# Transposes of the attention outputs: from TensorE through PSUM to DMA on 16-bit planes

## The chip, the cores and the metric

The kernel runs on one core of a Trainium2 chip as one launch. The metric is the device time of an execution in microseconds (us); lower is better. The kernel before takes 1124.64 us, the median of three runs (1124.45 to 1126.33).

## The reference

Attention with pooled queries feeds a channel-mixing MLP; all arrays are float32.

```python
# q, k, v: (8 batches, 8 heads, 1152, 64); x below: (8, 576, 512)
q_pool = q.reshape(B, H, S // 2, 2, D).mean(axis=3)          # 576 rows a head
scores = np.matmul(q_pool, k.transpose(0, 1, 3, 2)) / np.sqrt(D)
attn = softmax(scores)                                       # max subtracted, sum + 1e-9
x = np.matmul(attn, v).transpose(0, 2, 1, 3).reshape(B, 576, H * D)
x_prev = x shifted by one row (zeros ahead)
xk, xr = mu_k * x + (1 - mu_k) * x_prev, mu_r * x + (1 - mu_r) * x_prev
k = np.maximum(xk @ w_k, 0.0)                                # w_k 512 x 1024
out = sigmoid(xr @ w_r) * (k * k @ w_v)                      # w_v 1024 x 512, w_r 512 x 512
```

## The kernel before, in words

Every product is computed from fp16 pairs (a high part and a remainder), which is why each matrix product appears as several matmuls.

*Attention.* A head `n` (0 to 63) has six blocks of 96 pooled queries, 384 blocks in all. In `block`, TensorE (PE) writes the scores of a block into one of three PSUM tiles `s` (line 586), VectorE (DVE) takes the row maximum over keys into `mx` (593), PE transposes `mx` (596), DVE reduces again into `mb` (598), PE spreads it (625), ScalarE (ACT) writes it as an extra row of `qT` (628), PE adds the low score products (602), ACT takes the exponential into `pf` (635), and GpSimd (POOL) makes the low part `pl` from it (643). `window` multiplies 128 rows of weights with `v` (693, 695, 700) into the one PSUM bank `a`; `halves` (664) does the half window that two heads of a pair share.

*The pair's end.* Two heads form a pair; a batch has four pairs, the program 32. After the last window of a head, DVE (716, 718) takes the reciprocal of the sums and line 725 (721 on ACT in the first heads) normalises bank `a` into the SBUF tile `xb`, ten units of 64 columns. After the second head, `turns` runs: POOL copies one unit (734), PE transposes five 128x128 float32 pieces of `xb` into bank `a` (741), three, then two, and each group is copied from the bank into `xt` (750): a 64x64 and a 128x256 piece by ACT and a 64x64 piece by DVE from the first, a 128x256 piece by ACT from the second. The bank is taken until those copies are done. `xt` holds a batch transposed, channels on partitions, and has three buffers.

*MLP.* `ff` mixes tiles of 256 rows of `xt` (`mix`: 933, 936, 941, 944) and multiplies them with the weights (all at line 965), with `r`, `g` and `gl` between (992, 994, POOL 996). The weights are decoded in the first part of the program (836 to 854).

*The order.* Nothing is issued where it is written. Every operation is recorded with its engine, an estimated duration and its buffers (`op`), a planner (`Issue.run`) lays them out, a table of random moves (`MOVES`, with `SEED`) nudges the layout, and then each engine gets its instructions in that order. All engines work strictly through their own list. All loads, stores and DMA transposes are issued by SyncE (SP): loads (469, 515), transposes of keys and queries (535, 491), the copy `ks2` of the transposed keys (538) that the low score products read, stores (1032).

`SPREAD_MAX` is 0 and `NARROW` 32 in the kernel before, so the branches that they choose (`weigh`, `spread`) issue no instruction.

Of the kernel before, what the change touches and what calls it, by code (L numbers as in the profile page):

```python
# [11 lines left out]
F32 = mybir.dt.float32  # L12
F16 = mybir.dt.float16
# [8 lines left out]
P = 128  # L22
# [16 lines left out]
ROW = "Prelu"  # L39

# [12 lines left out]
KN_POOL, VT_POOL, XL_POOL = 0, 0, 0  # L53
# [7 lines left out]
SPREAD_MAX = 0  # L61
# [11 lines left out]
FIX_ACT = 1  # L73
FIX = 0.07
# [3 lines left out]
NARROW = 32  # L78
# [11 lines left out]
SEED, SPREAD = 2, 1.0  # L90
# [227 lines left out]
def kernel(  # L318
# [73 lines left out]
    vb = bufs("vb", NV, [P, NC, D + 8], F16)  # L392
# [3 lines left out]
    den, xb = bufs("den", 2, [P, NW], F32), bufs("xb", 1, [P, 2 * NW + 4, D], F32)  # L396
    xl_b = bufs("xlb", 1, [P, 3, D], F32)
# [29 lines left out]
    for t_ in qn:  # L427
        nc.gpsimd.memset(t_[:, 1, :, D:P] if SPREAD_MAX else t_[:, 1, :, 0:D], 0.0)
# [19 lines left out]
    def queries(n, key):  # L448
# [3 lines left out]
        l0 = 0 if n < SPREAD_MAX else D  # L452
# [57 lines left out]
    def prep(n, key):  # L510
# [26 lines left out]
        if n >= SPREAD_MAX:  # L537
            op("DMA", 0.54, lambda: nc.sync.dma_start(ks2[i][D:P], ks1[i][0:D]),
               r=[("ks1", i), ("ks1", i, 5)], w=[("ks2", i)], key=key + 1, load=0.65, more=0.15)
# [25 lines left out]
    def block(n, j, i, t):  # L565
# [10 lines left out]
        mxz, mbz = mx[z], mb[z]  # L576
# [12 lines left out]
        for c0, c1 in BK:  # L589
# [15 lines left out]
        if n < SPREAD_MAX:
            for c0, c1 in BK:
                op("PE", (c1 - c0) * 0.0430, lambda c0=c0, c1=c1: scores2(c0, c1),
                   r=[("ks1", hp), ("ks1", hp, 5)] + kl, w=[("s", z)], key=t + O_MAX)
            if FIX_ACT:
                op("ACT", 0.07, lambda: nc.scalar.activation(mbz, mbz, getattr(AF, ROW), scale=1.0 + EPS,  # L610
                                                             alpha=(1.0 - EPS) / (1.0 + EPS)),
                   r=[("mb", z)], w=[("mb", z)], key=t + O_MAX)
            else:
                op("DVE", FIX, lambda: nc.vector.scalar_tensor_tensor(
                    mbz, mbz, (1.0 + EPS) / (1.0 - EPS), mbz, op0=ALU.mult, op1=ALU.max),
                   r=[("mb", z)], w=[("mb", z)], key=t + O_MAX)

            def spread():
                for c0, c1 in BK:
                    nc.tensor.matmul(cols(c0, c1), mbz.broadcast_to([P, P]), negd[:, 0:c1 - c0].rearrange("p c q -> p (c q)"),  # L620
                                     start=False, stop=True, skip_group_check=True)

            op("PE", NC * QN / 2400 + 0.012, spread, r=[("mb", z)], w=[("s", z)], key=t + O_EXP)
        else:
            op("PE", 0.047, lambda: nc.tensor.matmul(s[:, 0:QN], mbz.broadcast_to([P, P]), negi[:, P - QN:P],  # L625
                                                     start=False, stop=False, skip_group_check=True),
               r=[("mb", z)], w=[("s", z)], key=t + O_MAX)
            op("ACT", 0.153, lambda: nc.scalar.activation(qlo[0:1], s[0:1, 0:QN], getattr(AF, ROW),  # L628
                                                          scale=1.0 - EPS, alpha=(1.0 + EPS) / (1.0 - EPS)),
               r=[("s", z)] + kl, w=qm, key=t + O_MAX)  # L630

            for c0, c1 in BK:
                op("PE", (c1 - c0) * 0.0430, lambda c0=c0, c1=c1: scores2(c0, c1),
                   r=[("ks2", hp)] + kl + qm, w=[("s", z)], key=t + O_EXP)
# [24 lines left out]
    def halves(n, t):  # L659
# [15 lines left out]
        x_ = xl_b[0][:, 0]  # L675
# [4 lines left out]
    def window(n, w, t):  # L680
# [72 lines left out]

    VW, MID = 2 * D + 1, NW - 1
    ROUND = [(0, 1, 2), (MID + 1, MID - 1, MID), (MID + 2, MID + 3, MID + 4)]
    UNIT = {MID: 2 * NW + 3, **{x: 2 * x + 2 for x in range(MID)}, **{MID + 1 + x: 2 * x + 3 for x in range(MID)}}

    def weigh(g, m, t):


        if m == MID:
            ps = [(2 * g, 0, HW, TQ), (2 * g + 1, HW, P, 0)]
        else:
            ps = [(2 * g + int(m > MID), 0, P, HW + (m if m < MID else m - MID - 1) * P)]
        us = [x for _, x0, x1, p0 in ps for x in range(p0 // U, (p0 + x1 - x0) // U)]
        pfk, plk = [("pf", x) for x in us], [("pl", x) for x in us]
        r_, y = [(r_, o.index(m)) for r_, o in enumerate(ROUND) if m in o][0]
        a0 = y * VW
        order = sorted(ROUND[r_])
        vk = [(x, n % NV, c0) for n, *_ in ps for x in ("vt", "vtl") for c0 in (0, *V_CUT)]  # L770
        k = range(NC)

        def mms(src, vs, c0, c1, v0):
            for c in range(c0, c1):
                for n, x0, x1, p0 in ps:
                    nc.tensor.matmul(a_b[x0:x1, a0 + v0:a0 + VW], src[:, c, p0:p0 + x1 - x0],
                                     vs[n % NV][:, c, 0:VW - v0],
                                     start=(m == order[0] and c == 0 and v0 == 0), stop=(v0 > 0 and c == NC - 1),
                                     skip_group_check=True)

        first = m == order[0]
        steps = [(0, 3), (3, 6), (6, NC)] if len(ps) == 1 else [(0, NC)]
        for c0, c1 in steps:
            op("PE", HALF * 0.65 if len(ps) > 1 else 3 * 0.0582, lambda c0=c0, c1=c1: mms(half(pf, F16, 1), vt, c0, c1, 0),
               r=vk + pfk + ([] if first and c0 == 0 else [ka]), w=[ka], key=t)
        for c0, c1 in [(0, 5), (5, NC)] if len(ps) == 1 else [(0, NC)]:
            op("PE", HALF * 0.35 if len(ps) > 1 else (c1 - c0) * 0.0306, lambda c0=c0, c1=c1: mms(pl, vb, c0, c1, D),
               r=[("vb", n % NV) for n, *_ in ps] + plk + [ka], w=[ka], key=t)
        if m < order[-1]:
            return  # L790

        b, h = divmod(2 * g, H)
        u = a_b[:, 0:3 * VW].rearrange("p (k x) -> p k x", x=VW)
        dz, x_ = den[r_ % 2][:, 0:3], xl_b[0]
        us = [UNIT[x] for x in ROUND[r_]]
        step = us[1] - us[0]
        op("DVE", 0.075, lambda: nc.vector.tensor_scalar(dz, u[:, :, 2 * D], GUARD, None, op0=ALU.add),
           r=[ka], w=[("den", r_ % 2)], key=t + O_EVAC)
        op("DVE", 0.08, lambda: nc.vector.reciprocal(dz, dz), r=[("den", r_ % 2)], w=[("den", r_ % 2)], key=t + O_EVAC)
        op("ACT", 0.051 + 3 * D / 1200, lambda: nc.scalar.copy(x_, u[:, :, 0:D]), r=[ka], w=[("xlb",)], key=t + O_EVAC)  # L800
        op("DVE", 0.07 + 3 * D / 960, lambda: nc.vector.tensor_tensor(
            u[:, :, D:2 * D], u[:, :, D:2 * D], x_, op=ALU.add), r=[ka, ("xlb",)], w=[ka], key=t + O_EVAC)
        op("DVE", 0.07 + 3 * D / 960, lambda: nc.vector.tensor_tensor(
            xb[0][:, us[0]:us[2] + 1:step], u[:, :, D:2 * D], dz.unsqueeze(2).broadcast_to([P, 3, D]), op=ALU.mult),
           r=[("den", r_ % 2), ka], w=[("xb", x) for x in us], key=t + O_EVAC)
        if r_ < 2:
            return
        turns(b, h // 2, 2 * NW + 2, t)
# [312 lines left out]
```

## Time and profile before

| what | value |
|---|---|
| median of three runs | 1124.64 us |
| span of the profiled execution | 1123.9 us |
| PE busy | 1086.5 us (97%) |
| DVE, ACT, POOL busy | 898.8, 841.5, 538.8 us |
| TensorE's granted clock, mean | 0.999 |

The span runs from the first to the last instruction; the execution that was profiled has no device time of its own in the results, so its span is set beside the median of the runs, which is 0.74 us longer. Busy is the union of the engine's instruction records. PE is the matmul itself, PEld the load of its stationary operand, which runs beside it. Matmuls overlap, so a record is longer than the distance from one matmul to the next.

### The profile page before, as it was taken

How to read it: one execution, taken by the hardware profiler on the slowest of the kernel's cores; microseconds unless marked ns; L12 is line 12 of the kernel's file. 1: busy time of each engine (PE TensorE's matmuls, PEld its weight loads, DVE VectorE, ACT ScalarE, POOL GpSimd, SP SyncE). 2: the span in 40 equal slices, each digit the busy share in tenths (PEclk: the TensorE clock that was granted, in tenths of full speed). 3: DMA queues.
4: the chain of work that ended last, by engine and by line, in shares of the span. 5: the costliest groups of instructions: out<-in, count | busy, mean ns of one | idle time of the engine just before them, and what ended most of it. 6: DMA issues, size and time to landing. Idle time of an engine off the chain costs nothing.

```text
span 1123.9 us, 44399 instructions
## 1 busy us (share of the span) xinstructions
PE 1086.5 (97%) x18956; PEld 891.4 (79%) x18956; DVE 898.8 (80%) x1660; ACT 841.5 (75%) x1794; POOL 538.8 (48%) x579
## 2 busy tenths in 40 slices
PE   6888899999999999999999999999999999999998
PEld 5777778888797878888697888888797978787565
DVE  7999979998987998789878788888878787874530
ACT  7999987778777687777867677778777776765743
POOL 4566665544364444555454544545453544542111
PEclk9999999999999999999999999999999999999999
DMA  8999756674455635553465454455564423410000
GB/s 207 260 208 210 170 102 145 160 149 101 105 119 127 128 69 119 101 132 100 87 146 107 103 118 102 104 128 98 120 123 102 89 76 76 75 28 11 20 20 29
DMA packets 218742, 125.69 MB, mean 112 GB/s; under 512 B 154032, under 2 KB 190896, under 8 KB 218544
## 3 DMA queue, kind: packets, MB, share of 16 engines
q1 hardware_dynamic: 218544, 122.86, 49.6%
q8 instruction: 148, 2.42, 0.9%
q14 instruction: 50, 0.41, 0.1%
HBM read 67.11 MB, written 9.44 MB: 68 GB/s over the span
## 4 chain that ended last, share of the span: by engine, by line
PE 53%; DVE 1%; issue 0%; ACT 0%; ACTq 0%; DVEq 0%
PE f L965 21%; PE s L602 6%; PE s L586 6%; PE s L965 4%; PE a L695 3%; PE a L700 3%; PE a L693 3%; PE a L965 2%; PE a L664 1%; PE s L596 1%; PE s L625 1%; PE a L741 1%; DVE mx L593 0%; DVE xlr L944 0%; DVE qn L480 0%
## 5 line engine op out<-in xcount | busy, mean ns | idle before, releaser
L643 POOL TENSOR_SCALAR pl<-pf 128x864 f16<-128x864 uint16 x384 | 382.1, 995 | 422.0 <-ACT pf L635 380.0
L593 DVE TENSOR_REDUCE mx<-s 128x96 f16<-128x864 f32 x384 | 400.8, 1053 | 78.9 <-PE s L586 49.0
L635 ACT ACTIVATE pf<-s 128x864 int32<-128x864 f32 x384 | 335.8, 883 | 84.7 <-PE s L602 60.3
L586 PE MATMUL s<-qT,ks 128*128 128x96 f16 x3456 | 224.0, 206 | 12.5 <-ACT pf L635 8.9
L602 PE MATMUL s<-qT,ks 128*128 128x96 f16 x3456 | 216.2, 206 | 2.9 <-ACT qT L628 2.7
L586 PEld LDWEIGHTS <-ks 128*128 128x128 f16 x3456 | 184.1, 98 | 40.4 <-issue 13.6
L602 PEld LDWEIGHTS <-ks 128*128 128x128 f16 x3456 | 179.2, 98 | 21.9 <-issue 4.0
L695 PE MATMUL a<-vt,pf 128*128 128x64 f16 x2304 | 192.3, 194 | 0.3 <-issue 0.3
L693 PE MATMUL a<-vt,pf 128*128 128x65 f16 x2304 | 191.8, 193 | 0.1
L693 PEld LDWEIGHTS <-pf 128*128 128x128 f16 x2304 | 161.2, 99 | 4.0 <-issue 0.4
L695 PEld LDWEIGHTS <-pf 128*128 128x128 f16 x2304 | 155.0, 97 | 4.7 <-issue 0.2
L628 ACT ACTIVATE qT<-s 1x96 f16<-1x96 f32 x384 | 87.2, 230 | 82.5 <-PE s L625 79.4
L598 DVE TENSOR_REDUCE mb<-s 128x1 f16<-128x128 f32 x384 | 109.1, 286 | 36.8 <-PE s L596 29.6
L965 PE MATMUL f<-xhk,wk_hi 128*128 128x256 f16 x496 | 135.2, 273 | 0.1
L965 PE MATMUL f<-xhk,wk_lo 128*128 128x256 f16 x496 | 135.2, 273 | 0.0
L965 PE MATMUL f<-xlk,wk_hi 128*128 128x256 f16 x496 | 135.2, 272 | 0.0
L700 PE MATMUL a<-vb,pl 128*128 128x65 f16 x2304 | 123.2, 193 | 0.8 <-issue 0.5
L996 POOL TENSOR_TENSOR gl<-g 128x512 f16<-128x512 f32 x72 | 76.1, 1057 | 88.3 <-ACT g L994 85.5
L965 PEld LDWEIGHTS <-wk_hi 128*128 128x128 f16 x1152 | 106.0, 98 | 10.2 <-issue 0.2
L700 PEld LDWEIGHTS <-pl 128*128 128x128 f16 x2304 | 97.6, 98 | 6.4 <-issue 0.6
L965 PE MATMUL f<-wv_hi,gl 128*128 128x512 f16 x240 | 91.0, 379 | 0.0
L965 PE MATMUL f<-wv_lo,g 128*128 128x512 f16 x240 | 90.9, 379 | 0.0
(117 smaller groups left out, 1988.4 us busy)
## 6 DMA issues: line engine op xcount, KB each, us to landing
kr<-in_k_dram SPq DMA_DIRECT2D x64, 288.0 KB
vr<-in_v_dram SPq DMA_DIRECT2D x64, 288.0 KB
qr<-in_q_dram SPq DMA_DIRECT2D x63, 256.0 KB
ks<-ks SPq DMA_DIRECT2D x64, 144.0 KB
out_dram<-em SPq DMA_DIRECT2D x36, 256.0 KB
xt<-in_moe_w_k_dram SPq DMA_DIRECT2D x8, 512.0 KB
xt<-in_moe_w_v_dram SPq DMA_DIRECT2D x8, 512.0 KB
qr<-in_q_dram SPq DMA_DIRECT2D x32, 64.0 KB
```

The costliest lines, as they stand in the source:

```text
L586: nc.tensor.matmul(cols(c, c + 1), ks1[hp][:, c, :], qhi, start=(c == c0), stop=False, skip_group_check=True)
L593: op("DVE", 0.975, lambda: nc.vector.tensor_reduce(mxz[:, P - QN:P], grid(0, NC).rearrange("p c q -> p q c"), axis=AX.X, op=ALU.max), r=[( ...
L598: op("DVE", 0.199, lambda: nc.vector.tensor_reduce(mbz, s[:, 0:P], axis=AX.X, op=ALU.max), r=[("s", z)], w=[("mb", z)], key=t + O_MAX)
L602: nc.tensor.matmul(cols(c, c + 1), (ks1 if n < SPREAD_MAX else ks2)[hp][:, c, :], qlo, start=False, stop=True, skip_group_check=True)
L628: op("ACT", 0.153, lambda: nc.scalar.activation(qlo[0:1], s[0:1, 0:QN], getattr(AF, ROW), scale=1.0 - EPS, alpha=(1.0 + EPS) / (1.0 - EPS) ...
L635: op("ACT", NC * QN / 1200 + 0.06, lambda: nc.scalar.activation(pf[:, :, rows], grid(0, NC), AF.Exp, bias=SHIFT, scale=0.125 / (2.0 * SQ)) ...
L643: op(pe, d, lambda: en.tensor_scalar(pl[:, :, rows], half(pf, U16, 0)[:, :, rows], LO, 1.0, op0=ALU.mult, op1=ALU.mult), r=[("pf", x) for ...
L693: nc.tensor.matmul(bank[:, a0:a0 + VN], half(pf, F16, 1)[:, c, rows], vt[jv][:, c, D:D + VN], start=(w == 1 and c == 0 and hh == 0), stop= ...
L695: nc.tensor.matmul(bank[:, a0:a0 + D], half(pf, F16, 1)[:, c, rows], vt[jv][:, c, 0:D], start=False, stop=False, skip_group_check=True)
L700: nc.tensor.matmul(bank[:, a0:a0 + VN], pl[:, c, rows], vb[jv][:, c, 0:VN], start=False, stop=(c == NC - 1), skip_group_check=True)
L965: nc.tensor.matmul(ps, terms[i][0], terms[i][1], start=(first and i == 0), stop=(i == last), skip_group_check=True)
L996: op("POOL", 2 * n * 0.00203 + 0.08, lambda f2=f2: nc.gpsimd.tensor_tensor(gl[:, f2, 0:n], g32[:, f2, 0:n], gh[:, f2, 0:n], op=ALU.subtrac ...
```

## The change

For pairs 5 to 31 (`CROSS = range(4, 31)`, counted from 0) `turns` hands over to `crossed`. POOL copies `xb`, seen as 16-bit words, into two planes `xp` (low halves and high halves), in two instructions. One DMA transpose on SP turns all ten 128x128 pieces of the two planes into `xd`. Three copies join the planes in `xt`: two of 64 partitions by ACT, one of 128 partitions by POOL. PE and bank `a` have no part in it. Pairs 1 to 4 and 32 keep the old way.

Beside that: `mx` has two buffers in place of three; the constant `negd` (one POOL instruction at the start), the unused branches and some spare columns are dropped; and the planner's table of moves is another one with another seed, so that every engine's list is laid out anew.

```diff
+CROSS = range(4, 31)
+SPLIT_ENG = "POOL"
+JOIN_ENG = "POOL"
+HALF_ENG = 'ACT'
+CROSS_LOAD, CROSS_MORE = 2.1, 0.5
...
-    44, 69, 70, 101, 134, 152, 174, 178, 265, 338, 388, 440, 473, 536, 539, 701, 728, 899, 906, 1027, 1054,
...
+    19, 49, 186, 236, 290, 409, 442, 580, 720, 1033, 1106, 1276, 1618, 2283, 5078, 5201, 6339, 9039, 9106,
...
-SEED, SPREAD = 2, 1.0
+SEED, SPREAD = 37, 1.0
...
-    mx, mb = bufs("mx", 3, [P, P], F16), bufs("mb", 3, [P, 1], F16)
+    mx, mb = bufs("mx", 2, [P, P], F16), bufs("mb", 3, [P, 1], F16)
+    xp, xd = bufs("xp", 1, [P, 2, 2 * NW, D], U16)[0], bufs("xd", 1, [P, 2, NW, P], U16)[0]
...
+    def crossed(b, g, t):
+        xu = xb[0].bitcast(U16).rearrange("p u (d t) -> p t u d", t=2)
+        yu = xt[b % 3][:, g].bitcast(U16).rearrange("p (q t) -> p t q", t=2)
+        for u1, u0, n_ in ((1, 1, 2 * NW - 1), (0, 1, 1)):
+            d, f = copier(SPLIT_ENG, 2 * D * n_)
+            op(SPLIT_ENG, d, lambda f=f, u0=u0, u1=u1, n_=n_: f(xp[:, :, u1:u1 + n_], xu[:, :, u0:u0 + n_]),
+               r=[("xb", x) for x in range(u0, u0 + n_)], w=[("xp", u1)], key=t + O_TURN)
+        op("DMA", 0.5, lambda: nc.sync.dma_start_transpose(
+            xd.rearrange("p t k x -> p (t k) x"), xp.rearrange("p t u d -> p (t u d)")),
+           r=[("xp", 0), ("xp", 1)], w=[("xd",)], key=t + O_TURN, load=CROSS_LOAD, more=CROSS_MORE)
+        free = [("xtf",)] if b % 3 == 2 else []
+        for y, ps, k0, k1, x0, x1, e in ((0, slice(0, HW), 0, 1, 0, HW, HALF_ENG), (1, slice(HW, P), 0, 1, HW, P, HALF_ENG),
+                                         (2, slice(0, P), 1, NW, 0, P, JOIN_ENG)):
+            n_ = (k1 - k0) * (x1 - x0)
+            d, f = copier(e, 2 * n_)
+            q0 = SPAN[y][0]
+            op(e, d, lambda f=f, ps=ps, k0=k0, k1=k1, x0=x0, x1=x1, n_=n_, q0=q0: f(
+                yu[ps, :, 1 + q0:1 + q0 + n_].rearrange("p t (k x) -> p t k x", k=k1 - k0), xd[ps, :, k0:k1, x0:x1]),
+               r=[("xd",)] + free, w=[("xt", b % 3, g, y)] + [("xt", b % 3, g, 3)] * (y == 2), key=t + O_TURN)
...
+        if b * NG + g in CROSS:
+            return crossed(b, g, t)
```

The order at the end of pair 13 shows the moved work on three engines. Line numbers differ between the two programs; the names of tiles carry buffer numbers.

PE before, at the first of the two groups of transposes: the pair's last score matmul, the transposes of `xb` into bank `a`, the transpose of `mx` of a later block, and MLP matmuls.

```order
L586 MATMUL s_133<-qT_88,ks_1_84 128x96
L741 MATMUL a<-ident,xb_105 128x128 x3
L596 LDWEIGHTS mx_99
L596 MATMUL s_135<-identb,mx_99 128x128
L965 LDWEIGHTS g_0_117
L965 MATMUL f<-wv_hi,g_0_117 128x512
```

PE of the change, between the last window of pair 13 and the first of pair 14 (593 is the transpose of `mx`, 913 the MLP, 583 the scores).

```order
L913 MATMUL f<-xhk_114,wk_hi 128x256
L593 LDWEIGHTS mx_96
L593 MATMUL s_132<-identb,mx_96 128x128
L913 LDWEIGHTS wk_hi
L913 MATMUL f<-xlk_112,wk_hi 128x256
L913 LDWEIGHTS wk_lo
L913 MATMUL f<-xhk_114,wk_lo 128x256
```

No transpose of `xb` stands there; MLP and score matmuls follow one another up to the next pair's window.

POOL before, at the same pair's end: 643 makes `pl`, 558 a part of `v`, 734 copies one unit of `xb`.

```order
L643 TENSOR_SCALAR pl<-pf 128x9x96
L734 COPY xb_105<-xb_105 128x64
L643 TENSOR_SCALAR pl<-pf 128x9x96 x7
L558 TENSOR_SCALAR vb_94<-vr_75 128x9x64
```

POOL of the change there: 719 are the two split copies, 730 the join, 619 makes `pl`, 944 makes `gl`.

```order
L719 COPY xp_104<-xb_102 128x2x576
L619 TENSOR_SCALAR pl<-pf 128x9x96 x2
L719 COPY xp_104<-xb_102 128x2x64
L944 TENSOR_TENSOR gl_117<-g_0_116 128x512
L619 TENSOR_SCALAR pl<-pf 128x9x96
L944 TENSOR_TENSOR gl_117<-g_0_116 128x512
L730 COPY xt_106<-xd_105 128x2x512
L619 TENSOR_SCALAR pl<-pf 128x9x96 x2
```

Three copies stand where one stood, with `pl` and `gl` queued between and behind them.

SP before, near the same pair: the transpose of keys (535), their copy `ks2` (538), loads and a store.

```order
L515 DMA vr_74<-in_v_dram 128x576
L535 DMA_TRANSPOSE ks_0_83<-kn_79 128x9x128
L538 DMA ks_0_85<-ks_0_83 64x1152
L515 DMA kr_73<-in_k_dram 128x576
```

SP of the change: 533 is the transpose of keys, 721 that of the planes, 535 the copy of the keys.

```order
L533 DMA_TRANSPOSE ks_0_81<-kn_77 128x9x128
L721 DMA_TRANSPOSE xd_105<-xp_104 128x10x128
L535 DMA ks_0_83<-ks_0_81 64x1152
L513 DMA vr_73<-in_v_dram 128x576
```

The new transpose stands between the keys' transpose and their copy, and what follows it on SP waits for it to be issued.

## Rows read from the trace of the kernel before

**Rows 1.** The page: span, and busy time of each engine.

```profile
span 1123.9 us, 44399 instructions
PE 1086.5 (97%) x18956; PEld 891.4 (79%) x18956; DVE 898.8 (80%) x1660; ACT 841.5 (75%) x1794; POOL 538.8 (48%) x579
```

**Rows 2.** Stretches: length, busy us of PE, PEld, DVE, ACT, POOL; clock, DMA.

```profile
0.00:150.00 150.00, 121.93 (x2536) 107.21 (x2537) 132.22 (x243) 138.50 (x305) 93.64 (x101) 1.00 0.92 209
150.00:1036.00 886.00, 880.43 (x15898) 732.90 (x15897) 737.73 (x1360) 658.03 (x1395) 432.73 (x466) 1.00 0.48 104
1036.00:1124.00 88.00, 84.16 (x526) 51.25 (x524) 28.86 (x58) 45.01 (x96) 12.47 (x12) 0.99 0.07 25
```

**Rows 3.** Line 741, the transposes: duration ns min/median/max.

```profile
L741 PE MATMUL a<-ident,xb x160: 272/273/329, 44.3 to 1036.2; 128*128 128x128 f32 x160
```

**Rows 4.** Timeline around the two groups of pair 31: start us, length us.

```profile
1007.68 0.51 PE L741 MATMUL a<-ident,xb 128*128 128x128 f32 x3
...
1008.03 0.55 PE L586 MATMUL s<-qT,ks 128*128 128x96 f16 x9
...
1010.22 0.38 PE L741 MATMUL a<-ident,xb 128*128 128x128 f32 x2
...
1010.43 0.21 PE L625 MATMUL s<-negi,mb 128*128 128x96 f16 x1
```

**Rows 5.** Waits of PE and PEld, 150 to 1036 us: total, times, longest.

```profile
PE s L625 <- DVE mb L598: 2.9, 5, 1.0
...
PE a L741 <- DVE xt L750: 0.5, 1, 0.5
...
PEld L625 <- DVE mb L598: 5.9, 11, 1.2
...
PEld a L741 <- DVE xt L750: 1.4, 4, 1.0
```

**Rows 6.** Groups by form: busy us, mean ns, idle before. Copies out of bank a.

```profile
L750 ACT COPY xt<-a 128x256 f32<-128x256 f32 x64 | 23.3, 365 | 3.1 <-PE a L741 1.3 <-PE s L625 1.1 <-DVE em L1029 0.4
...
L750 DVE COPY xt<-a 64x64 f32<-64x64 f32 x32 | 7.3, 228 | 4.3 <-ACT xt L750 3.4
```

**Rows 7.** Three POOL lines: duration ns min/median/max.

```profile
L643 POOL TENSOR_SCALAR pl<-pf x384: 910/911/1893, 15.8 to 1026.9; 128x864 f16<-128x864 uint16 x192
...
L558 POOL TENSOR_SCALAR vb<-vr x56: 670/670/1056, 93.2 to 989.8; 128x576 f16<-128x576 f32 x56
...
L996 POOL TENSOR_TENSOR gl<-g x72: 1038/1040/1510, 141.7 to 1106.0; 128x512 f16<-128x512 f32 x72
```

**Rows 8.** Groups of `pl` on POOL and of its reader on PE, as above.

```profile
L643 POOL TENSOR_SCALAR pl<-pf 128x864 f16<-128x864 uint16 x384 | 382.1, 995 | 422.0 <-ACT pf L635 380.0 <-PE s L602 11.4 <-PE a L700 6.3
...
L700 PE MATMUL a<-vb,pl 128*128 128x65 f16 x2304 | 123.2, 193 | 0.8 <-issue 0.5 <-POOL pl L643 0.3
```

**Rows 9.** Two DVE lines, two SBUF inputs: groups (mean ns), then min/median/max.

```profile
L547 DVE SCALAR_TENSOR_TENSOR vt<-vr,vt 128x576 f16<-128x576 f32 x64 | 59.0, 922 | 1.3 <-ACT vt L543 1.3
...
L944 DVE TENSOR_TENSOR xlr<-xm,xhr 128x256 f16<-128x256 f32 x72 | 39.6, 558 | 4.2 <-ACT xhr L941 3.9
...
L547 DVE SCALAR_TENSOR_TENSOR vt<-vr,vt x64: 718/752/1596, 15.1 to 992.2; 128x576 f16<-128x576 f32 x64
...
L944 DVE TENSOR_TENSOR xlr<-xm,xhr x72: 390/418/1204, 121.5 to 1092.0; 128x256 f16<-128x256 f32 x72
```

**Rows 10.** Timeline of SP: the keys' transpose, the copy behind it.

```profile
323.50 1.29 SPq L535 DMA_TRANSPOSE ks<-kn  x1
...
327.75 0.47 SPq L538 DMA_DIRECT2D ks<-ks  x1
```

**Rows 11.** Timeline near 512 us: start, length, idle before, releaser.

```profile
511.90 2.29 POOL L643 TENSOR_SCALAR pl<-pf 128x864 f16<-128x864 uint16 x2 [1.25 <-ACT pf L635]
...
511.93 1.48 DVE L480 SCALAR_TENSOR_TENSOR qn<-qs,qn 128x576 f16<-128x576 f32 x1
...
513.80 0.22 PE L625 MATMUL s<-negi,mb 128*128 128x96 f16 x1 [0.98 <-DVE mb L598]
```

More of the change, by code (lines that the diff above doesn't have):

```diff
@@ L52 @@
 LATE, SLACK = 0.04, 0.05
-KN_POOL, VT_POOL, XL_POOL = 0, 0, 0
+KN_POOL = 0
+XL_POOL = 0
 DEC_K, DEC_RV = "V", "V"
@@ L427 @@
     for t_ in qn:
-        nc.gpsimd.memset(t_[:, 1, :, D:P] if SPREAD_MAX else t_[:, 1, :, 0:D], 0.0)
+        nc.gpsimd.memset(t_[:, 1, :, 0:D], 0.0)
     for t_ in mx:
@@ L451, in queries @@
         i, u = n // 2 % 2, n // 2 % N_QN
-        l0 = 0 if n < SPREAD_MAX else D
+        l0 = D
         qv = q[b, h:h + 2].rearrange("h (t f) d -> h t (f d)", f=2)
@@ L536, in prep @@
                r=[(x, m, c) for x in ("kn", "knl") for c, _ in KC], w=[("ks1", i), ("ks1", i, 5)], key=key + 1, load=1.9, more=T_MORE)
-        if n >= SPREAD_MAX:
-            op("DMA", 0.54, lambda: nc.sync.dma_start(ks2[i][D:P], ks1[i][0:D]),
-               r=[("ks1", i), ("ks1", i, 5)], w=[("ks2", i)], key=key + 1, load=0.65, more=0.15)
+        op("DMA", 0.54, lambda: nc.sync.dma_start(ks2[i][D:P], ks1[i][0:D]),
+           r=[("ks1", i), ("ks1", i, 5)], w=[("ks2", i)], key=key + 1, load=0.65, more=0.15)
         for c0, c1 in zip((0, *V_CUT), (*V_CUT, NC)):
@@ L575, in block @@
         rows, us = slice(p0, p0 + QN), range(p0 // U, (p0 + QN) // U)
-        mxz, mbz = mx[z], mb[z]
+        mxz, mbz, y = mx[i % 2], mb[z], i % 2
         def cols(c0, c1):
@@ L601, in scores2 @@
             for c in range(c0, c1):
-                nc.tensor.matmul(cols(c, c + 1), (ks1 if n < SPREAD_MAX else ks2)[hp][:, c, :], qlo,
+                nc.tensor.matmul(cols(c, c + 1), ks2[hp][:, c, :], qlo,
                                  start=False, stop=True, skip_group_check=True)
[L605 to L634, printed above, removed]
@@ new lines, in block @@
+        op("PE", 0.047, lambda: nc.tensor.matmul(s[:, 0:QN], mbz.broadcast_to([P, P]), negi[:, P - QN:P],
+                                                 start=False, stop=False, skip_group_check=True),
+           r=[("mb", z)], w=[("s", z)], key=t + O_MAX)
+        op("ACT", 0.153, lambda: nc.scalar.activation(qlo[0:1], s[0:1, 0:QN], getattr(AF, ROW),
+                                                      scale=1.0 - EPS, alpha=(1.0 + EPS) / (1.0 - EPS)),
+           r=[("s", z)] + kl, w=qm, key=t + O_MAX)
@@ L635, in block @@
+        for c0, c1 in BK:
+            op("PE", (c1 - c0) * 0.0430, lambda c0=c0, c1=c1: scores2(c0, c1),
+               r=[("ks2", hp)] + kl + qm, w=[("s", z)], key=t + O_EXP)
         op("ACT", NC * QN / 1200 + 0.06, lambda: nc.scalar.activation(
@@ L728, in window, with copier, turns @@
         if hh:
-            turns(b, g, 0, t)
-    def turns(b, g, u0, t):
-        op("POOL", 0.2, lambda: nc.gpsimd.tensor_copy(xb[0][:, u0], xb[0][:, u0 + 1]), r=[("xb", u0 + 1)], w=[("xb", u0)],
+            turns(b, g, t)
+    def copier(e, n):
+        return {"POOL": (0.12 + n * 0.00113, nc.gpsimd.tensor_copy), "ACT": (0.093 + n / 1200, nc.scalar.copy),
+                "DVE": (0.07 + n / 960, nc.vector.tensor_copy)}[e]
+    def crossed(b, g, t):
[17 more added lines that the diff above has]
+               r=[("xd",)] + free, w=[("xt", b % 3, g, y)] + [("xt", b % 3, g, 3)] * (y == 2), key=t + O_TURN)
+    def turns(b, g, t):
+        if b * NG + g in CROSS:
+            return crossed(b, g, t)
+        op("POOL", 0.2, lambda: nc.gpsimd.tensor_copy(xb[0][:, 0], xb[0][:, 1]), r=[("xb", 1)], w=[("xb", 0)],
            key=t + O_EVAC)
-        units = [u0] + [2 * k_ for k_ in range(1, NW)]
+        units = [2 * k_ for k_ in range(NW)]
         x_ = xt[b % 3][:, g]
@@ L752, in turns @@
                    r=[ka] + ([("xtf",)] if b % 3 == 2 else []), w=[("xt", b % 3, g, y), ("ar",)], key=t + O_TURN)
[L754 to L808, printed above, removed]
@@ L1049 @@
                 kq = (n * NB) * PER + O_PREP - 5.0
-                if SPREAD_MAX and 0 <= n + 1 - SPREAD_MAX < 2 * N_QN:
-                    u_ = (n + 1) // 2 % N_QN
-                    op("POOL", 0.6, lambda u_=u_: nc.gpsimd.memset(qn[u_][:, 1, :, 0:D], 0.0),
-                       w=[("qnl", u_, c) for c in range(NQ)], key=kq)
                 queries(n + 1, kq)
```

24 lines of the change are left out of this document (9 added, 15 removed), and 3 rows, old and new, of the table AHEAD2.

## The prediction, made before the changed kernel was run

> **What bounds the kernel now.** The page first: PE is busy for 1086.5 of 1123.9 us, DVE for 898.8, ACT for 841.5 and POOL for 538.8 [rows 1]. Such shares are means over stages with different limits, so the next view is the busy time by stretch [rows 2]. From 150 to 1036 us, while attention and MLP run together, PE is busy for 880.4 of 886 us; DVE has 148 us to spare there, ACT 228 and POOL 453. From 1036 on only MLP is left and PE is busy for 84.2 of 88 us. Ahead of 150 us PE is busy for 121.9 of 150 while ACT is busy for 138.5: that stage is not PE's. So in 974 of the 1124 us a microsecond of PE work is a microsecond of time, and the span shows little else to win: PE stands still for 5.6 us in the middle, 28 at the start and 4 at the end. The clock was granted in full (1.00, that is 2.4 GHz) in the first two stretches and at 0.99 in the last.
>
> **What the change removes.** Of the 160 transposes of line 741, five a pair, 27 pairs lose theirs: 135. What one costs is not its record. A record lasts 273 ns [rows 3], but matmuls overlap. Around pair 31 the group of three starts at 1007.68 and the next instruction at 1008.03; the group of two starts at 1010.22, the next at 1010.43 [rows 4]. A pair thus holds PE for 0.35 + 0.21 = 0.56 us, 0.112 a transpose. 27 x 0.56 = **15.1 us**, all in the stretch in which PE is the bound. The copies out of bank a go too. In that stretch PE waited for one of them 0.5 us, and the weight loads ahead of a transpose 1.4 us [rows 5]; I take off **1.0 us**, with 0.5 and 1.4 as ends. ACT gets rid of two copies of 365 ns a pair and DVE of one of 228 ns [rows 6]: 20 and 6 us in all, on engines with room, so these count for nothing by themselves. ACT takes two small copies a pair in their place, shorter than those they replace, at nothing for the same reason; should ACT lose its 228 us of room they would cost what they last, about 0.2 us each by the nearest row, the 228 ns of the 64x64 copy [rows 6].
>
> **What it adds.** No row shows a copy of 16-bit words on POOL. Its split takes 2 x 576 and 2 x 64 elements a partition, its join 2 x 512: 2304 in three instructions. Two one-operand lines of POOL are near: 576 elements in 670 ns and 864 in 911 ns [rows 7], so 0.84 ns an element and 188 ns for the instruction: 1.15 + 0.30 + 1.05 = 2.5 us a pair. The two-operand line, 512 elements in 1040 ns, gives 2.03 ns an element and 4.7 us. I take the lower, since a copy has one operand and line 643 reads 16-bit words at the same stride. 27 pairs make 67 us (127 at the upper end): POOL goes from 539 to 606 (666) us, 55 to 60% of the new span. By itself that is hidden: POOL waits 422 us ahead of line 643, and PE waited 0.3 us for `pl` in the whole run [rows 8].
>
> **What POOL does to DVE.** A DVE instruction with two SBUF inputs stands still while POOL runs. Line 944 takes 418 ns in the median and 558 in the mean, up to 1204; line 547 752, 922 and 1596 [rows 9]. The excess is 72 x 0.14 + 64 x 0.17 = 21 us on these two lines, over 539 us of POOL. Other lines of that kind exist, line 944's twin for the other weights among them, so I reckon once to three times that, 0.04 to 0.12 us of DVE for each us of POOL: the added 67 (127) us cost DVE 3 to 15 us, against the 6 that it is rid of. DVE stays near 84% of the middle stretch. Part of this reaches PE, through the row maximum: PE's loads waited 5.9 us for `mb`, PE itself 2.9 [rows 5], beside the 21 to 65 us of DVE held up. That is at most 0.28 us of PE for each us of DVE, so 0 to 4 us more; I take **1.0 us**. The Trainium skill (SBUF — State Buffer, section Who interferes with whom) says that a VectorE instruction with two SBUF inputs and a GpSimd instruction that reads SBUF exclude each other for a whole instruction; these rows agree, 1204 against 418 ns.
>
> **What it moves.** The pair's result reaches `xt` later: by the split, the DMA and the join. The keys' transpose of nine pieces was issued at 323.50 and the copy that needs it at 327.75 [rows 10], 4.25 us; ten pieces should take about as long, and up to twice that (8.5) where other transfers lie ahead. With 2.5 us of POOL and its queue I expect some 8 to 15 us from `xb` to `xt`. What hides it is the MLP's backlog: 88 us of MLP are left when attention ends [rows 2], so the tile that waits for a new pair is not the next one due. Without that cover PE would lose these 8 to 15 us once a batch. In the order the new transpose stands on SP ahead of the copy of the keys, so that copy, and the loads behind it, wait for POOL's second split, which has two `pl` ahead of it: 2 to 3 us. The low score products wait for that copy; the leading waits of PE and its loads in the middle stretch are for DVE [rows 5], so I put nothing. The third `mx` buffer saves a wait only where the reduction of line 593 runs three blocks ahead; DVE, not PE, would stand, for one or two instructions of PE, and I put nothing. `negd` and the dead branches are nothing either.
>
> **The new order.** The table of moves cannot be priced from rows. It bounds itself: at best it closes the 37 us in which PE stands still, 28 of them in the start that the change hardly touches; at worst it opens a like amount. I put zero for the likeliest and 5 us to either side.
>
> **The sum.** -15.1 - 1.0 + 1.0 = -15.1 us. The profiled execution spans 1123.9 us, which gives 1108.8; the median of the runs is 0.74 longer, and with the same around it I predict **1109.5 us**, 1.35% less. Its own range is 1104 to 1115: the 5 us of the order, with the bounds above inside them.
>
> **The rivals.**
>
> *POOL's long copies hold DVE, and PE pays.* Near 512 us this is seen whole: two `pl` run on POOL for 2.29 us (twice 0.911 alone [rows 7]), a DVE instruction that started with them takes 1.48 us, `mb` behind it is late, and PE waits 0.98 us [rows 11]. A split or a join is one instruction of 1.05 to 1.15 us, longer than a `pl`, and there are 54. At 0.98 us each, 15 such waits eat the gain. Half of that, 8, gives 1117; one a pair, 27, gives 1109.5 + 26.5 = **1136**, slower than before; it turns slower at 18 (over 0.2%). Against it: 384 `pl`, 72 `gl` and 56 `vb` of near that length cost PE and its loads only 5.9 us now. I give 0.15 to a gain cut to between 1115 and 1122 by this or by late planes, and 0.05 to slower.
>
> *The freed PE time is not used.* If the loop from scores over `mx`, `mb` and exponential set the pace, PE would idle for what it is rid of and the time would stay at **1124**. For it: DVE at 83% of the middle. Against it: PE's 5.6 us of idle time in 886. I give 0.04.
>
> *More than the sum.* If the new order also fills part of the start, say a quarter to a half of the 37 us, the time is **1091 to 1100**; with a smaller part, 1100 to 1104. For it: bank a is free for about 2.75 us more a pair (from 1007.68 to 1010.43 in pair 31), so windows can move. Against it: the middle has nothing to fill. 0.13, most of it above 1100.
>
> *A transpose costs its whole record.* 135 x 0.273 = 36.9 us, **1088**. The starts 0.11 us apart speak against it. 0.02. The Trainium skill (TensorE: Matmul & The Clock Gate, Part 4: PE-mode transpose) gives about 275 ns for a transpose in a kernel; 135 of these, an estimate, are 37 us too. The record of 273 ns agrees with it, but as a price on a queue that runs ahead the distance of starts decides.
>
> That the change does not do what it says is out: in the order no transpose of pair 13 is left on PE.
>
> **How the numbers follow.** Forecast 0.61, more than the sum 0.13, smaller gain 0.15, unused 0.04, slower 0.05, whole record 0.02. The range 1101 to 1119 leaves out the whole record, somewhat under half of the fuller case, a third of the smaller gain, and the two cases without a gain: 0.02 + 0.05 + 0.05 + 0.09, about 0.2. A measurement of this kernel tells a change from none at about 0.2%, 2.2 us. Faster by more than that: 0.61 + 0.13 + 0.15 + 0.02 = 0.91; within it 0.04; slower 0.05.
>
> **What would show it.** Right: 25 transposes left on line 741's successor, PE busy falling by about as much as the span, PE still over 98% of its middle stretch, POOL busy near 600 us, the split near 1.15 us and the join near 1.05 in their minimum, the new DMA landing in 4 to 8 us. Wrong: PE idle in the middle above 10 us, with waits for `mb` or for `pl` behind a join; a start stage that is longer or shorter by more than 5 us; medians of the POOL copies near 2 us and more.

## The result, and the profile after

The changed kernel takes **1111.87 us**, the median of 4 runs (1109.3 to 1112.62), against 1125.28 for the kernel before on the same chip. The ratio is 0.9877, 95% interval 0.9863 to 0.9891: faster by 13.4 us. Timed again in a later job it gave 1111.57 and 0.9873 (0.9854 to 0.9891).

The page, to be read beside [rows 1]: span, then busy time, share and instructions of each engine.

```profile
span 1110.4 us, 44176 instructions
PE 1070.5 (96%) x18821; PEld 877.6 (79%) x18821; DVE 905.3 (82%) x1632; ACT 836.8 (75%) x1767; POOL 615.9 (55%) x632
```

PE has 135 matmuls and 16.0 us of busy time less, and the span is 13.5 us shorter. POOL gains 77 us. DVE should have lost the 6 us of its copies out of bank `a`; it gained 6.5.

The same stretches as [rows 2].

```profile
0.00:150.00 150.00, 119.76 (x2536) 106.41 (x2537) 131.56 (x242) 137.65 (x302) 93.91 (x101) 1.00 0.92 211
150.00:1036.00 886.00, 880.20 (x15855) 728.82 (x15853) 750.97 (x1350) 664.01 (x1395) 511.32 (x522) 1.00 0.55 114
1036.00:1111.00 75.00, 70.56 (x436) 42.33 (x433) 22.79 (x41) 35.11 (x71) 10.62 (x11) 1.00 0.06 22
```

The middle is as full as it was (880.2 against 880.4 of 886 us), at the full clock. The time that PE got back shows at the end, where 75 us are left in place of 88. In the first stretch PE did the same number of matmuls.

The new operations and what is left of the old one, by line (duration in ns: min/median/max).

```profile
L746 PE MATMUL a<-ident,xb x25: 272/273/332, 46.4 to 1022.2; 128*128 128x128 f32 x25
...
L730 ACT COPY xt<-xd x54: 320/342/353, 176.8 to 998.8; 64x128 uint16<-64x128 uint16 x54
L730 POOL COPY xt<-xd x27: 1330/1354/1755, 169.4 to 997.3; 128x1024 uint16<-128x1024 uint16 x27
...
L721 SPq DMA_TRANSPOSE xd<-xp x27: 1253/1356/2312, 163.7 to 992.1; - x27
```

Twenty-five transposes are left on PE. The join, which reads two planes and writes every second word, has a median of 1.35 us.

The groups by form tell the two split copies apart from the join (busy us, mean ns, then idle time before).

```profile
L730 POOL COPY xt<-xd 128x1024 uint16<-128x1024 uint16 x27 | 37.1, 1376 | 7.1 <-DMA xd<-xp 6.0
L719 POOL COPY xp<-xb 128x1152 uint16<-128x1152 uint16 x27 | 34.3, 1271 | 10.2 <-DVE xb L701 9.3
L719 POOL COPY xp<-xb 128x128 uint16<-128x128 uint16 x27 | 10.7, 395 | 1.3
```

That is 82 us for the three, 3.0 us a pair, where 2.5 were reckoned. POOL gained only 77 in all, because 27 of its copies of one `xb` unit went (line 734 before, 237 ns in the median, 6 us). One of the split copies beside a DVE instruction, on the timeline (start, length, idle before):

```profile
476.28 1.15 POOL L719 COPY xp<-xb 128x1152 uint16<-128x1152 uint16 x1 [0.41 <-DVE xb L701]
476.33 1.71 DVE L524 TENSOR_TENSOR kn<-kr,kn 128x576 f16<-128x576 f32 x1
...
477.05 0.55 PE L583 MATMUL s<-qT,ks 128*128 128x96 f16 x9
...
477.96 1.04 DVE L590 TENSOR_REDUCE mx<-s 128x96 f16<-128x864 f32 x1
```

Line 524 has a median of 0.75 us; started 0.05 us behind the split, it takes 1.71, about 1 us more. The scores for the reduction behind it are there at 477.60, and it starts at 477.96, so about 0.4 us of that reach it.

The DMA transpose and the join that waited for it, pair 30:

```profile
964.41 1.27 SPq L721 DMA_TRANSPOSE xd<-xp  x1
...
967.83 1.35 POOL L730 COPY xt<-xd 128x1024 uint16<-128x1024 uint16 x1 [0.17 <-DMA xd<-xp]
```

From issue to reader 3.4 us, ten pieces where the keys' nine took 4.25 [rows 10]; it is the shortest such distance of the 27 pairs, for most joins wait for POOL's own queue. POOL waited for such a transfer 6.0 us in all, ACT 0.8, PE never.

What PE itself waited for between 150 and 1022 us (total, times, longest), to be set against [rows 5]:

```profile
PE s L583 <- ACT pf L611: 3.7, 4, 1.6
PE s L602 <- DVE mb L595: 0.7, 2, 0.4
PE f L913 <- ACT r L940: 0.5, 1, 0.5
PE s L599 <- ACT qT L605: 0.3, 1, 0.3
```

The kernel before had, besides the lines of [rows 5]:

```profile
PE s L586 <- ACT pf L635: 0.9, 2, 0.5
```

The wait for `mb` has fallen from 2.9 to 0.7, that for `pf` has grown from 0.9 to 3.7; the bank is not in the list.

### The profile page after: what moved, and what is told of

The parts are those of the page before. It is cut to its first block, busy times and chain, and to the rows that moved or that the text cites. A ratio compares the mean times of both kernels' runs of the same rounds, so it can differ in the third digit from the quotient of the medians.

```text
span 1110.4 us, 44176 instructions
## 1 busy us (share of the span) xinstructions
PE 1070.5 (96%) x18821; PEld 877.6 (79%) x18821; DVE 905.3 (82%) x1632; ACT 836.8 (75%) x1767; POOL 615.9 (55%) x632
## 4 chain that ended last, share of the span: by engine, by line
PE 62%; DMA 2%; DVE 1%; ACT 1%; issue 1%; POOL 0%; SPq 0%; ACTq 0%; DVEq 0%
PE f L913 25%; PE s L583 8%; PE s L599 8%; PE s L913 4%; PE a L676 4%; PE a L671 4%; PE a L669 4%; PE a L913 2%; PE a L640 2%; PE s L593 1%; DMA ks<-kn 1%; DMA qT<-qn 1%; PE s L602 1%; ACT pf L611 1%; DVE mx L590 0%
## 5 line engine op out<-in xcount | busy, mean ns | idle before, releaser
L583 PE MATMUL s<-qT,ks 128*128 128x96 f16 x3456 | 217.4, 207 | 15.1 <-ACT pf L611 14.0
L599 PE MATMUL s<-qT,ks 128*128 128x96 f16 x3456 | 212.5, 206 | 3.8 <-ACT qT L605 3.0
L583 PEld LDWEIGHTS <-ks 128*128 128x128 f16 x3456 | 182.2, 98 | 41.6 <-issue 19.2
L599 PEld LDWEIGHTS <-ks 128*128 128x128 f16 x3456 | 177.0, 98 | 23.7 <-issue 5.8
L913 PE MATMUL f<-wv_hi,g 128*128 128x512 f16 x240 | 91.0, 379 | 0.0
```

Of the source, the lines that this page charges most:

```text
L583: nc.tensor.matmul(cols(c, c + 1), ks1[hp][:, c, :], qhi, start=(c == c0), stop=False, skip_group_check=True)
L599: nc.tensor.matmul(cols(c, c + 1), ks2[hp][:, c, :], qlo, start=False, stop=True, skip_group_check=True)
L913: nc.tensor.matmul(ps, terms[i][0], terms[i][1], start=(first and i == 0), stop=(i == last), skip_group_check=True)
```

## The experiments

Differences are between ratios to the kernel before, times 1125 us; each ratio stands with its interval.

**1. Only PE's transposes out of the kernel before, in its own order.** The copies out of bank `a` stay.

```diff
-                for k_ in range(t0, t1):
+                for k_ in range(t0, t1) if b * NG + g not in range(4, 31) else ():
```

> The kernel before, in its own order, with the PE transposes of line 741 left out for pairs 5 to 31 (135 of 160); the copies out of bank a stay and copy what stands there, so the output is not the reference's. Nothing is added on POOL or SP. Theory (PE time is time, one for one; POOL, DVE and DMA hide the rest): 135 x 0.109 to 0.112 = 14.7 to 15.1 us less than before, plus up to 1.4 us of waits ahead of transposes: about 1109 to 1111. Rival (the copies on POOL hold DVE and cost about 3 us or more of the gain): 17 to 20 us less, 1105 to 1108, clearly below the changed kernel. Rival (the new order made the gain): under 8 us less, over 1117.

1119.86 us, ratio 0.9947 (0.9931 to 0.9963): 6 us, not 15, in the range set for the rival that the new order made the gain (experiments 2, 6 and 7 speak against that one). PE's waits, 150 to 1022 us, say where part of the rest went:

```profile
PE s L625 <- DVE mb L598: 3.1, 4, 1.0
PE s L596 <- DVE mx L593: 2.9, 7, 0.8
PE s L602 <- ACT qT L628: 0.8, 2, 0.6
```

The wait for `mx` was 0.2 us before; the loads ahead of those two lines waited 8.1 and 6.7 us (5.9 and 2.4). PE reached its next score work sooner and found the reductions not done; all of PE's waits in this view come to 8.6 us, against 4.9 before. The rest of the loss shows only in the distances between matmuls, further below.

**2. The 135 transposes put back into the changed kernel,** five at the head of the next pair's first window, reading a constant, with no copy behind them.

```diff
+            if w == 1 and hh == 0 and c0 == 0 and n // 2 in range(5, 32):
+                for k_ in range(5):
+                    nc.tensor.transpose(a_b[:, k_ % 3 * P:(k_ % 3 + 1) * P], ident, ident)
```

> The changed kernel, in its own order, with five 128x128 float32 transposes (of the identity, into bank a) put back on PE for each of 27 pairs, at the head of the next pair's first window, which overwrites them. Nothing else changes, and they wait for nothing that the window does not wait for. Theory: 14.7 to 15.1 us more than the changed kernel, 1126 to 1127, so about the kernel before. Rival (the new order made the gain, PE has room): less than 8 us more, under 1120. Rival (a transpose costs its record of 273 ns): 37 us more, 1149.

1124.81 us, ratio 0.9981 (0.9968 to 0.9994): 11.7 us more than the changed kernel. The group by form:

```profile
L670 PE MATMUL a<-ident 128*128 128x128 f32 x135 | 19.4, 274 | 0.0
```

Records of 274 ns would make 37 us. From one start to the next they take 14.9 us together (median 109 ns), and the time rose by most of that: 11.7 us, or 0.09 a transpose, somewhat under the 14.7 to 15.1 expected. The price by starts nearly stands, and the 37 us of the whole records are refuted. The runs spread from 1120.52 to 1126.88, and the profiled one took 1121.41. Its span is only 8.8 us longer than the changed kernel's, but its start was 3.4 us shorter, where the two programs do not differ (the table below, last row); from the end of pair 5's normalisation to the last matmul it took 12.2 us more.

**3. Split and join left out for 19 of the 27 pairs** (13 to 31), in the changed order.

> The changed kernel, in its own order, with the two split copies and POOL's join left out for pairs 13 to 31 (19 of 27); the DMA transpose and ACT's two copies stay, the MLP then reads older rows of xt, so the output is not the reference's. POOL loses about 19 x 3 = 57 us. Theory: 0 to 1.5 us less than the changed kernel. Rival (POOL holds DVE, DVE holds PE): 3 us less or more, which would be the missing part of the forecast.

```diff
-            op(SPLIT_ENG, d, lambda f=f, u0=u0, u1=u1, n_=n_: f(xp[:, :, u1:u1 + n_], xu[:, :, u0:u0 + n_]),
+            op(SPLIT_ENG, d, lambda f=f, u0=u0, u1=u1, n_=n_: None if b * NG + g > 11 else f(xp[:, :, u1:u1 + n_], xu[:, :, u0:u0 + n_]),
```

The join's line is changed alike. 1108.35 us, ratio 0.985 (0.983 to 0.987): about 3 us less than the changed kernel by the medians, and the two intervals overlap a little. DVE and POOL on the page:

```profile
PE 1068.8 (97%) x18821; PEld 876.5 (79%) x18821; DVE 892.0 (81%) x1632; ACT 835.8 (76%) x1767; POOL 557.2 (50%) x575
```

DVE is rid of 13.3 us without having lost an instruction: that is what the copies held it up. The time is another matter. The two programs are alike up to pair 13, and the normalisation of pair 5 shows that the profiled execution was ahead before anything was left out, first the changed kernel, then this one:

```profile
160.58 0.49 DVE L701 TENSOR_TENSOR xb<-a,den 128x320 f32<-128x320 f32 x1
157.09 0.49 DVE L701 TENSOR_TENSOR xb<-a,den 128x320 f32<-128x320 f32 x1
```

Of the 5.1 us between the two spans, 3.5 lie there, where the programs do not differ: in seven profiled executions with this order, all alike up to that point, the normalisation ends between 157.6 and 162.2 us. What moves it is not known. From pair 5's to pair 12's the two take 214.5 and 214.6 us. From pair 12's to the last matmul, where the copies are left out, it is 730.6 us in the changed kernel, 729.4 in its second execution, and 728.8 here. By these traces 19 pairs' copies cost 0.6 to 1.8 us; an estimate for all 27 is 1 to 3. Between the theory (0 to 1.5 us) and the rival (3 or more) the medians alone do not decide, and the traces lean to the theory.

**4. Split and join issued twice.** The same two lines, with `for _ in range(2)` around the copy.

> The changed kernel, in its own order, with the two split copies and POOL's join issued twice for all 27 pairs: about 80 us more on POOL, DVE held 3 to 15 us longer. Theory: 0 to 3 us more than the changed kernel. Rival (POOL's copies cost PE time): 5 us more or over, up to 1 us for each of the 54 long copies.

1127.26 us, ratio 1.0008 (0.9997 to 1.0019): 14.7 us more, which uses up the whole gain; the theory of 0 to 3 us failed. The page:

```profile
PE 1072.8 (95%) x18821; PEld 877.7 (78%) x18821; DVE 926.6 (82%) x1632; ACT 837.2 (74%) x1767; POOL 702.8 (62%) x713
```

PE's waits from 150 to 1022 us:

```profile
PE s L583 <- ACT pf L611: 7.3, 11, 1.4
PE s L599 <- ACT qT L605: 2.7, 5, 1.0
PE a L640 <- POOL pl L619: 1.9, 1, 1.9
PE s L602 <- DVE mb L595: 1.9, 5, 0.6
```

And ACT's first operation of the MLP, in the same stretch, which waits for no join in the changed kernel:

```profile
ACT tmp L881 <- POOL xt L730: 6.0, 5, 2.0
```

POOL is 87 us busier, DVE 21 us. Of PE's waits 1.9 us in this list are for POOL's own product `pl`; most are for `pf`, `qT` and `mb`. But ACT's `pf` in its turn waited 7.5 us for POOL in the whole span, against 2.4 in the changed kernel. So DVE's reductions and a late POOL both stand behind these waits, and this run alone does not part them.

**5. POOL as busy, but with memsets.** A memset of the same region ahead of each of the three POOL copies, which writes SBUF and reads none.

> The changed kernel, in its own order, with a POOL memset of the same region ahead of each of the 81 copies (2 x 576, 2 x 64 and 2 x 512 words), so that POOL gets about as much more to do as in the run with every copy twice; but a memset reads nothing from SBUF. The output stays the reference's. Theory (a POOL instruction that reads SBUF holds up DVE's two-input instructions, and PE pays for that): DVE busy stays near the 905 us of the changed kernel instead of 927, and the time rises by 0 to 5 us, to 1112 to 1117. Rival (what counts is that POOL itself is late, with pl, gl and the join behind): 10 to 15 us more, as with every copy twice, 1122 to 1127.

1116.44 us, ratio 0.9918 (0.9905 to 0.9931): 4.6 us more. The page:

```profile
PE 1071.7 (96%) x18821; PEld 876.8 (79%) x18821; DVE 913.2 (82%) x1632; ACT 836.4 (75%) x1767; POOL 680.2 (61%) x713
```

POOL is 64 us busier, three quarters of experiment 4, for a third of its price by the ratios, and DVE 8 us in place of 21. (From the end of pair 5's normalisation to the last matmul, which leaves the start out, the price is 5.8 us against 13.5.) So DVE's loss hangs in the main on what POOL's instructions read. That the time goes the same way is argued, not shown: a memset needs neither `xb` nor the planes, so it ran in part where POOL would have stood waiting for them (15.3 us in the changed kernel, 4.3 here, 24.3 in experiment 4). `pf` waited as long for POOL as there (8.3 us), but `tmp` only 2.2 us for a join and not 6.0. The Trainium skill (SBUF — State Buffer, section Who interferes with whom) says that a VectorE instruction with two SBUF inputs contends with a GpSimd instruction that reads SBUF and not with one that only writes; the two runs agree in direction, though the memsets were not quite free.

**6 and 7. Both kernels with an empty table of moves,** so that neither profits from a search.

> The kernel before with its table of moves emptied: the planner's own order, not searched. Theory: slower than before by 3 to 10 us, 1128 to 1136. It is read against the changed kernel without moves.

> The changed kernel with its table of moves emptied. Theory (the change itself is worth 14.7 us of PE less what POOL's copies cost through DVE, about 8): 5 to 10 us under the kernel before without moves. Rival (the copies cost next to nothing once the planner lays the program out around them): 13 to 16 us under it. Rival (the search made the gain): within 3 us of it.

Before: 1133.23 us, ratio 1.0071 (1.0057 to 1.0085). Changed: 1113.85, ratio 0.9888 (0.9872 to 0.9904). The change is worth 21 us between these, more than between the searched orders and more than the theory (5 to 10) or the first rival (13 to 16) had it, so the new search is not where the gain comes from.

**8. The DMA transposes of pairs 13 to 31 left out.**

> The changed kernel, in its own order, with the DMA transposes of pairs 13 to 31 left out (19 of 27); the copies stay, the join reads older planes, so the output is not the reference's. Theory: within 1.5 us of the changed kernel, since transfers and SP have room and no PE wait of its profile names them. Rival (late planes hold POOL in the join, and PE behind it): 3 us less or more.

1112.77 us, ratio 0.9883 (0.9868 to 0.9897): no difference. The transfer and SP's part are hidden.

**9. As 1, but laid out anew:** no moves, and the planner told that these transposes take no time.

```diff
+            keep = b * NG + g not in range(4, 31)
...
-                for k_ in range(t0, t1):
+                for k_ in range(t0, t1) if keep else ():
...
-            op("PE", 0.113 * (t1 - t0), turned, r=[("xb", x + z) for x in units[t0:t1] for z in (0, 1)], w=[ka], key=t + O_TURN)
+            op("PE", 0.113 * (t1 - t0) if keep else 0.0, turned, r=[("xb", x + z) for x in units[t0:t1] for z in (0, 1)], w=[ka], key=t + O_TURN)
```

> The kernel before without moves, with the PE transposes of pairs 5 to 31 left out and told to the planner as work of no time, so that every list is laid out around the freed PE time (the run in the fixed order of before gave 6 us for them). The copies out of bank a stay, the output is not the reference's. It is read against the kernel before without moves, 1133.2. Theory (PE time is time once the lists are laid out anew): 13 to 16 us less, 1117 to 1120; the rest of the way to 1113.9 of the changed kernel without moves is what bank a and its copies cost. Rival (DVE and ACT hold PE back whatever the order): 5 to 8 us less, 1125 to 1128.

1126.32 us, ratio 1.001 (0.9997 to 1.0022): 7 us below experiment 6, the kernel that it is to be set against, and 13.7 above experiment 7. My theory, that a new layout would let PE use the time, failed: the gain stays at the 6 to 7 us of experiment 1. The waits of PE, 150 to 1022 us, are again for the reductions and what follows them:

```profile
PE s L582 <- ACT pf L631: 3.0, 8, 0.7
PE s L592 <- DVE mx L589: 2.7, 7, 0.8
PE s L621 <- DVE mb L594: 2.0, 5, 0.6
PE s L598 <- ACT qT L624: 1.3, 3, 0.5
```

**10. Split and join on ACT,** with moves searched for it.

> The changed kernel with the two split copies and the join on ACT in place of POOL, with a seed and a table of moves of its own. Theory (POOL's copies hold up DVE, ACT's do not): DVE busy falls from 905 to about 890 us, POOL back to about 530, and the time is 3 to 8 us under the changed kernel, 1104 to 1109, and under the next kernel, which keeps POOL and was searched as long. Rival (ACT is late with pf and PE waits for it): no better than the next kernel, 1110 or more.

1115.04 us, ratio 0.9907 (0.9892 to 0.9921): 3.4 us more than on POOL; theory failed, rival held. The page:

```profile
PE 1072.3 (96%) x18821; PEld 879.4 (79%) x18821; DVE 895.9 (80%) x1632; ACT 895.0 (80%) x1848; POOL 533.0 (48%) x551
```

DVE is rid of 9 us, but ACT has 58 more; in the middle PE waited 3.3 us for `qT` and 1.9 for `r` (0.3 and 0.5 in the changed kernel).

**11. The changed kernel with another searched table of moves.**

> The changed kernel with another seed and another table of moves alone, searched as long as that of the kernel with ACT's copies. Theory: within 3 us of the changed kernel, 1108 to 1114: what is left is not a matter of luck in the order. Rival (the order of the changed kernel was a poor one): 5 us less or more.

1109.76 us, ratio 0.9864 (0.9847 to 0.9881), in a job in which the changed kernel itself gave 0.9873 (0.9854 to 0.9891). It has the lowest median of all full versions, but is not told apart from the changed kernel.

## Why the prediction was right, and where its working was not

The time (1111.87 for 1109.5), the sign and the mechanism came as predicted: 25 transposes are left, PE's busy time fell by 16.0 us and the span by 13.5, and PE is busy for 99.3% of the middle. Of the other signs, the split's minimum is 1.14 us as said, but the join's is 1.33 and not 1.05, and the transfer landed 3.4 to 5.1 us after its issue (24 of the 27, median 3.7), more than half of them under the 4 to 8. Experiments 1 and 9 show that one step under the sum was too simple.

**Where the time went on PE.** To see this I took, from the trace, the distance from each matmul's start to the next one's. For the transposes these are summed. For every other matmul the excess over the median of its kind in the kernel before is summed, once for the stretches from 1 us before to 6 us after the normalisation that ends one of pairs 5 to 31, and once for the rest of the time between the first and the last of these (the middle). The second execution is that of the later job; the last row is counted from the span's start.

| us, one profiled execution each | before | exp. 1 | changed | changed, second execution | exp. 2 | exp. 3 | exp. 6 | exp. 9 | exp. 7 | exp. 4 | exp. 5 |
|---|---|---|---|---|---|---|---|---|---|---|---|
| transposes (of `xb`; in exp. 2 also of the constant) | 21.3 | 3.8 | 4.7 | 4.3 | 19.7 | 4.8 | 21.2 | 5.1 | 5.4 | 4.7 | 4.7 |
| lost by others, pair ends | 6.0 | 15.8 | 4.7 | 5.0 | 3.7 | 4.3 | 10.2 | 19.4 | 5.6 | 5.7 | 5.9 |
| lost by others, rest of middle | 15.9 | 17.3 | 19.1 | 18.0 | 17.3 | 17.9 | 17.6 | 18.8 | 18.7 | 31.6 | 23.7 |
| first to last matmul | 1116.0 | 1109.1 | 1100.6 | 1099.8 | 1109.7 | 1095.9 | 1125.5 | 1115.5 | 1102.6 | 1115.4 | 1104.5 |
| pair 5's normalisation ends at | 166.0 | 165.3 | 161.1 | 161.1 | 157.7 | 157.6 | 168.9 | 165.8 | 162.1 | 162.2 | 159.1 |

**Step one, "a microsecond of PE work is a microsecond of time".** This is what failed, as a rule. Without the transposes alone (experiment 1) PE was rid of 17.5 us and lost 9.8 again at the pair ends; laid out anew (experiment 9 against 6) it was rid of 16.1 and lost 9.2. At a pair's end bank `a` is closed: from the end of the normalisation to the first matmul of the next window pass 6.25 us in the mean before, 5.96 in experiment 1, 6.21 in 9, but 2.38 in the changed kernel and 2.33 in 7. While it is closed PE has only scores and MLP, and the scores wait for DVE's reductions; the transposes filled 0.56 us of just that gap. In experiment 1 the end of pair 28 reads like this:

```profile
901.60 0.48 DVE L725 TENSOR_TENSOR xb<-a,den 128x320 f32<-128x320 f32 x1
...
907.05 0.35 ACT L750 COPY xt<-a 128x256 f32<-128x256 f32 x1
...
908.26 0.22 PE L625 MATMUL s<-negi,mb 128*128 128x96 f16 x1 [0.91 <-DVE mb L598]
...
908.91 0.19 PE L693 MATMUL a<-vt,pf 128*128 128x65 f16 x1
```

And in the changed kernel:

```profile
898.04 0.48 DVE L701 TENSOR_TENSOR xb<-a,den 128x320 f32<-128x320 f32 x1
...
900.05 0.19 PE L669 MATMUL a<-vt,pf 128*128 128x65 f16 x1
```

The normalisation ends at 902.08 and 898.52; the next window starts 6.8 us later there, with a wait of 0.91 on the way, and 1.5 us later here. The sum's 15.1 came out only because the transposes went together with the copies that keep the bank. The step did not ask for that, so in this much its number was luck; it is far off for the transposes alone. Between experiments 9 and 7, 13.8 of the 13.9 us that PE's other matmuls lost less in the middle lie at the pair ends, and the times differ by 13.7. Experiment 2 closes the square: with the transposes on PE and the bank open after 2.92 us the pair ends lost 3.7 us, and from there taking the transposes out is worth most of their 14.9. Taking them out gives 6 us with the bank closed and 11.7 with it open. That the open bank is the cause is read from these distances and not isolated, for the two pairs of kernels differ in POOL's copies and in the order too; the kernel before with an earlier bank alone, or a second bank, was not run, and which of the copies' length, their place on ACT and DVE, or the order around them keeps it closed so long stays open.

**The transposes, 15.1 us.** 16.6 by the distances, 16.0 of busy time, 11.7 when they are put back: right within some 3 us, and the rival of the whole record falls with experiment 2.

**Waits for bank `a`, 1.0 us.** In the change as made, the pair ends lost 1.3 us less (1.0 in the second execution). Right in size, but for a reason that the step did not name: nearly all of the bank's worth is that it keeps the gap from growing once the transposes are gone.

**POOL's copies, 67 us, and DVE's hold, 1.0 us of the path.** The copies took 82 us, chiefly since the join took 1.35 us and not 1.05; POOL gained 77, for the prediction had not taken off the 27 copies of one `xb` unit that went. DVE came out 12.7 us above 898.8 - 6.2, in the upper part of the 3 to 15. On the path the rest of the middle lost 3.2 us more than before, 2.0 in the second execution, and experiment 3 puts the copies' share at 1 to 3 us (estimate). So the 1.0, with 0 to 4 as ends, was right or a little low. The first rival, DVE held up by POOL, is thus real for DVE and small for the time; experiment 4 shows how near it was, for a second helping of the same copies costs 14.7 us. How much of that goes through DVE and how much through late planes and a late `pl` stays open.

**Late planes, SP's queue, ACT's small copies at nothing.** Experiment 8 shows the transfer and SP's part at nothing. From the end of the normalisation to the end of POOL's join pass 8.7 to 16.1 us, 11.6 in the mean, much as the 8 to 15 had it. ACT's took 342 ns and not 228, and ACT still had 222 us to spare in the middle.

**The order, zero with 5 us to either side.** PE's first matmul starts at 5.54 us in place of 3.81, because the new order has PE transpose the first keys ahead of the first queries (experiment 11's starts at 3.80). That is no loss in itself: those keys were transposed at 5.75 before, and the first scores start at 8.34 now and at 9.31 before. In the account by distances the start and everything outside the middle cost 1.0 us more together (+1.7 and -0.7), less than the 4.6 us by which the start differs between executions of one order. Experiments 6 and 7 bound the rest: the search had gained 8 us for the kernel before and about 1 for the changed one.

**What came together.** -16.6 (transposes) - 1.3 (pair ends) + 3.2 (rest of the middle) - 0.7 (outside it) + 1.7 (start) is -13.7, the span's 13.5 within 0.2. The span is 1.6 us above the forecast's 1108.8: the rest of the middle (2.2 above its 1.0) and the start with what is outside (1.0) were dearer, transposes and pair ends gave 1.8 more (1.4 together). No one term can be blamed for that: such sums of one execution move by some 2 us, and the changed kernel's own runs spread over 3.3. The other 0.7 us of the 2.4 is that the median lies 1.5 us above the profiled span, where the forecast added 0.74.

## What to carry to other kernels

Price a removed operation together with the buffer that it occupies, and test both: leaving out the TensorE work alone gave 6 us, putting it alone back cost 12, and what separated the two was how long a PSUM bank stayed closed. An operation in a gap that does not shrink costs little there, even on an engine that is 99% busy: 17.5 us of PE time left out of such gaps gave 6. Before moving copies to a GpSimd that has room, look at which two-input VectorE instructions run beside them and at what is queued behind them: here a first helping cost 1 to 3 us by estimate and a second 15. And before an effect of 3 us is read from two medians, set marks in the traces: here as much lay ahead of the first instruction that differed.

## What the runs showed of the hardware that was not expected

A GpSimd copy and a GpSimd memset of the same region are not alike to the rest of the core: 87 us more of copies made DVE 21 us busier and the kernel 14.7 us longer, 64 us more of memsets 8 and 4.6. What of the difference in time is POOL's own lateness was not parted (experiment 5).

ACT copied 64x128 16-bit words from SBUF to SBUF in 342 ns, though the 128x256 float32 copy out of PSUM that it replaced took only 365 [rows 6], and it did the split in 1.14 us and the join in 1.35 in the mean (experiment 10), no faster than POOL undisturbed (1.15 and 1.35). For strided copies of 16-bit words the two engines cost the same here.
